# Gate and up weights in one tile, and their 256-column matmuls merged into 512-column ones

## Chip, cores and metric

One core of a Trainium2 chip. The metric is the device time of one execution in microseconds (us), lower is better. The kernel before takes 268.47 us (median of 3 runs, 268.25 to 269.01).

## The reference

An S5 layer (a diagonal complex recurrence over 2048 tokens of 1024 values) and a small mixture step are applied to the layernorm of x, and everything is added up. The change touches only the mixture step: a router picks 2 of the 2048 tokens, and a gated expert with an inner width of 3584 runs on these two rows.

```python
def _B_ref(x, w_r, w_gate, w_up, w_down):        # x: the layernorm's output, (1, 2048, 1024)
    r = x @ w_r
    idx = jnp.argsort(-r, axis=-1)[:, :2]        # two tokens
    ...
    g = _silu(x_sel @ w_gate)                    # w_gate, w_up: 1024 x 3584, bf16
    u = x_sel @ w_up
    y = (g * u) @ w_down                         # w_down: 3584 x 1024
    ...                                          # times sigmoid(r), added into the two rows
    return x + upd.reshape(B, S, D)

xn = _layernorm(A_x)
return A_x + _A_ref(xn, ...) + _B_ref(xn, ...)   # _A_ref: the recurrence
```

## The kernel before

Two parts matter. The first is how the expert's matmuls are laid out. Only two rows of activations exist, padded to 32, so they would fill a quarter of the array's columns. The kernel therefore cuts the weight's columns into four pieces and lets each piece be multiplied in its own strip of 32 array columns (`tile_position=(0, 32 * q)`), with the activations as the stationary operand and the weights streaming. Gate and up are done in 14 blocks (`UPV`): three parts of 1024 weight columns, each in four steps of 256 of the 1024 inputs, and one part of 512 columns in two steps of 512 inputs. The down product follows in 7 blocks.

```python
NREP = 4
UPB = [(b, DH * 2, 2, DT // 2) for b in range(0, F - DH, 2 * DH)] + [(F - DH, DH, 4, DT // 4)]
UPV = [(i, k) for i, blk in enumerate(UPB) for k in range(blk[3])]
...
wpool = ctx.enter_context(tc.tile_pool(name="wpool", bufs=4))     # each tile 512 KB
...
def load_w(n):                                   # n even: gate, n odd: up, then down
    if n < NUP:
        (b, k), w = UPV[n // 2], (B_w_gate, B_w_up)[n % 2]
        f0, fw, nk, _ = UPB[b]
        wt = wpool.tile([128, nk, fw], BF16, name="wt", tag="w")
        nc.sync.dma_start(out=wt[:], in_=w[k * nk * 128:(k + 1) * nk * 128, f0:f0 + fw].rearrange(...))
    ...

def moe_gateup(v):                               # 16 (or 32) matmuls a block
    ...
    wt = [ms.pop(("w", 2 * v + m)) for m in range(2)]
    for a in range(nk):
        j = k * nk + a
        for m in range(2):                       # gate, up
            for q in range(NREP):                # four strips
                nc.tensor.matmul(out=ms["pG", b][32 * q:32 * q + 32, m, :], lhsT=ms["xselT"][:, j, :],
                                 rhs=wt[m][:, a, q * fq:(q + 1) * fq], start=(j == 0 and m == 0),
                                 stop=(j == DT - 1 and m == 1), tile_position=(0, 32 * q))
```

The second part is the order. A list scheduler, run when the kernel is built, takes each piece of work with an estimated duration, a key, its predecessors and the ring of buffers it needs, and from these decides where on each engine it stands. The keys have been tuned by hand and search (`ADJUST`). A changed estimate or ring can thus move other work.

```python
for n in range(NW):                              # 42 loads; mb: megabytes that hold the DMA queue
    add(("w", n), "SP", 0.8, lambda n=n: load_w(n), ..., key=20 + n,
        takes=[("w", n, [("mm", n // 2)])], mb=0.43)
for v in range(NV):                              # 21 blocks
    ...
    add(("mm", v), "PE", 0.55, ..., [("w", 2 * v), ("w", 2 * v + 1)] + src + ..., key=-40 + v)
```

Of the kernel before, what the change touches and what calls it, by code (L numbers as in the profile page):

```python
# [12 lines left out]
BF16 = mybir.dt.bfloat16  # L13
# [10 lines left out]
NREP = 4  # L24
# [54 lines left out]
class Plan:  # L79
# [10 lines left out]
    def add(self, name, eng, dur, fn, deps=(), key=0.0, takes=(), mb=0.0, lag=0.0):  # L90
        assert name not in self.tasks, name
        key += self.adjust.get(name[0], 0.0) + self.adjust.get(name, 0.0)
        self.tasks[name] = dict(eng=eng, dur=dur, fn=fn, deps=list(deps), key=key, takes=list(takes), mb=mb, lag=lag)
# [70 lines left out]
def kernel(  # L164
# [18 lines left out]
    nc = tc.nc  # L183

    ctx.enter_context(tc.manual_schedule())
    _, L, D = A_x.shape
# [5 lines left out]
    DT = D // 128  # L192
# [6 lines left out]
    UPB = [(b, DH * 2, 2, DT // 2) for b in range(0, F - DH, 2 * DH)] + [(F - DH, DH, 4, DT // 4)]  # L199
    UPV = [(i, k) for i, blk in enumerate(UPB) for k in range(blk[3])]  # L200
# [69 lines left out]

    pl = Plan(ADJUST)
    for tag, n in (("xt", 4), ("xn", 2), ("xnT", NF - 2), ("pT", 1), ("pB", 3), ("pY", 3), ("u", 2), ("v", 2), ("gf", 2),
                   ("gb", 2), ("hT", 3), ("xr", 2), ("xa", 1), ("ot", 2), ("w", 4)):
        pl.ring(tag, n)
    add = pl.add

# [146 lines left out]
    for i in range(NWARM):  # L423
        add(("warm", i), "PE", 0.224 if i < 24 else 0.15, keep_clock, [("warm", i - 1)] if i else [], key=100 + i,
            takes=[("pB", "warm", [("warm", NWARM - 1)])])
# [4 lines left out]
    for c in range(NCH):  # L430
# [28 lines left out]
        if c < PE_T:  # L459
            add(("Tpe", c), "PE", 0.48, lambda c=c: transpose_pe(c), [("apply", c)], key=ln - 10,  # L460
                takes=[("pY" if c < 4 and c % 2 else "pT", ("T", c), [("xnT", c)])] + ([("pY", ("T", 0), [("xnT0",)])] if c == 0 else []))
# [192 lines left out]

    xrp = ctx.enter_context(tc.tile_pool(name="xrp", bufs=2))
    outp = ctx.enter_context(tc.tile_pool(name="outp", bufs=2))
    wpool = ctx.enter_context(tc.tile_pool(name="wpool", bufs=4))


    v_tiles = {}  # L660
# [86 lines left out]
    for c in range(NCH):  # L747
        f = c // CPF
        for js in parts(c):
            k = js.start  # L750
            half = len(parts(c)) > 1
            d = (js.stop - js.start) / PT
# [12 lines left out]
            for ri in range(2):  # L765
# [3 lines left out]
                    takes=[gb_take] if c == NCH - 1 else [("gf", (c, k), [("gb", c, k, i) for i in range(2)] + cy[0] + cy[1])] if half else  # L769
# [5 lines left out]
            if c + 1 < NCH:  # L775
# [4 lines left out]
                takes=[("hT", c, [("Y", c, YLAST(c))])])  # L780
# [50 lines left out]
    for c in range(NCH):  # L831
        add(("xr", c), "SP", 0.8, lambda c=c: load_xr(c), key=c - 2, deps=[("B", PT - 1, 1)] if c < 4 else [("Y", c - 4, 0)],
            takes=[("xr", c, [("xa", c)])], mb=0.25)
# [6 lines left out]
        wd = [(d.stop - d.start) / DH for d in cols(c)]  # L840
# [18 lines left out]
    ms = moe_state  # L859
# [92 lines left out]
    def sel_xT():  # L952
# [20 lines left out]
        takes=[("xt", "mw", [("gT", len(UPB) - 1), ("mm", len(UPV) - 1)])])  # L973


    NUP = 2 * len(UPV)

    def load_w(n):
        if n < NUP:
            (b, k), w = UPV[n // 2], (B_w_gate, B_w_up)[n % 2]  # L980
            f0, fw, nk, _ = UPB[b]
            wt = wpool.tile([128, nk, fw], BF16, name="wt", tag="w")
            nc.sync.dma_start(out=wt[:], in_=w[k * nk * 128:(k + 1) * nk * 128, f0:f0 + fw].rearrange("(a di) f -> di a f", di=128))
        else:
            fp = n - NUP
            wt = wpool.tile([128, 2, D], BF16, name="wd", tag="w")
            nc.sync.dma_start(out=wt[:], in_=B_w_down[fp * 256:(fp + 1) * 256, :].rearrange("(a fi) d -> fi a d", fi=128))
        ms["w", n] = wt

    def moe_gateup(v):  # L990
        b, k = UPV[v]
        f0, fw, nk, kn = UPB[b]
        fq = fw // NREP
        if k == 0:
            ms["pG", b] = psum.tile([128, 2, fq], F32, name="pG", tag="T" if b % 2 else "misc")
        wt = [ms.pop(("w", 2 * v + m)) for m in range(2)]
        for a in range(nk):
            j = k * nk + a
            for m in range(2):
                for q in range(NREP):  # L1000
                    nc.tensor.matmul(out=ms["pG", b][32 * q:32 * q + 32, m, :], lhsT=ms["xselT"][:, j, :],  # L1001
                                     rhs=wt[m][:, a, q * fq:(q + 1) * fq], start=(j == 0 and m == 0), stop=(j == DT - 1 and m == 1),
                                     tile_position=(0, 32 * q))

    def moe_exp(b):
        e = ms["e"][:, 0:UPB[b][1] // NREP]
# [25 lines left out]
    def moe_down(v):  # L1032
        if v == 0:
            ms["pD"] = psum.tile([128, DQ], F32, name="pD", tag="misc")
        for h in range(2):
            wd = ms.pop(("w", NUP + 2 * v + h))
            for a in range(2):
                ft = 4 * v + 2 * h + a
                for q in range(NREP):
                    nc.tensor.matmul(out=ms["pD"][32 * q:32 * q + 2, :], lhsT=ms["guT"][:, ft, :],  # L1040
                                     rhs=wd[:, a, q * DQ:(q + 1) * DQ], start=(ft == 0), stop=(ft == FT - 1),
                                     tile_position=(0, 32 * q))
# [17 lines left out]
    NV = NW // 2  # L1060
    for n in range(NW):
        add(("w", n), "SP", 0.8, lambda n=n: load_w(n), [("C", NDH - 1, 1)], key=20 + n,
            takes=[("w", n, [("mm", n // 2)])], mb=0.43)
    for v in range(NV):
        up = v < len(UPV)
        if up:
            b, k = UPV[v]
            src = [("xT",)] + ([("gT", b - 2)] if b > 1 and k == 0 else [])
        else:
            src = sorted({("gT", min((4 * (v - len(UPV)) + i) // 8, len(UPB) - 1)) for i in range(4)})  # L1070
        add(("mm", v), "PE", 0.55, (lambda v=v: moe_gateup(v)) if up else (lambda v=v: moe_down(v - len(UPV))),
            [("w", 2 * v), ("w", 2 * v + 1)] + src + ([("mm", v - 1)] if v else []), key=-40 + v)
    for b, (f0, fw, nk, kn) in enumerate(UPB):
        last = max(v for v, bk in enumerate(UPV) if bk[0] == b)
        d = fw / (2 * DH)
# [5 lines left out]
        takes=[("xt", "ym", [("row_", q) for q in range(1, NREP)]), ("xt", "ymb", [("Y", NCH - 1, YLAST(NCH - 1))])])  # L1081
# [36 lines left out]
```

## Time and profile before

| | before |
|---|---|
| span of the profiled execution | 266.8 us |
| PE busy | 259.1 us (97%) |
| DVE busy | 243.1 us (91%) |
| first gate/up matmul (tile pG) starts | 152.57 us |
| last matmul of the kernel starts | 263.57 us |
| gate/up matmuls: 192 of 256 columns, 64 of 128 | 7.3 and 1.3 us busy |

In the lines of this document, PE is the matmul engine (TensorE), DVE the VectorE, ACT the ScalarE and SP the engine whose queue issues the loads. On DVE, u is the recurrence's input (from pB), v its rotation, gf and gb the result of the scans, hT the rotation back, which PE multiplies into pY; ot takes pY to the output. Chunks and blocks are counted from 0. "128*32 128x256 x192" is a form: the stationary operand is 128 by 32, the moving one 128 by 256, and there are 192. L1001 is the source line of the gate/up matmul, L629 the input product (pB), L815 and L808 the output product (pY), all three in the full-array form (128*128); L1021 (pU) is a transposition in that form too, L1040 or L1041 (pD) the down product in the strip form. The three lines on the gate/up matmuls, from the view of the groups by form, give busy time and mean duration in ns; PEld is the loading of the stationary operand:

```profile
L1001 PE MATMUL pG<-wt,mw 128*32 128x256 bf16 x192 | 7.3, 275 | 0.0
L1001 PE MATMUL pG<-wt,mw 128*32 128x128 bf16 x64 | 1.3, 220 | 0.0
L1001 PEld LDWEIGHTS <-mw 128*32 128x32 bf16 x256 | 5.0, 96 | 4.3 <-issue 4.2
```

These matmuls hold PE for less than 9 of 267 us, so the change works on 3% of the span. The two lines of the PE timeline that bound the part the change can move:

```profile
152.57 1.06 PE L1001 MATMUL pG<-wt,mw 128*32 128x256 bf16 x32
...
263.57 0.28 PE L817 MATMUL pY<-ymb,hot 2*128 2x256 bf16 x1
```

From start to start this **stretch** is 263.57 - 152.57 = 111.00 us. The 111.00 rests on one profile of the kernel before.

### The profile page before, as it was taken

What the parts mean: (1) busy time and instruction counts of PE and PEld (TensorE: products, weight loads), DVE (VectorE), ACT (ScalarE), POOL (GpSimd) and SP (SyncE); (2) the same over time, 40 slices, a digit from 0 to 9 for tenths busy, and PEclk for the clock granted to TensorE, in tenths of its full rate; (3) what the DMA queues carried; (4) which work ended last, traced back from release to release, by engine and by line L of the source; (5) the groups of instructions that cost most, each with busy time, mean ns of one, the idle gap of its engine ahead of it and who ended that gap; (6) DMA issues with size and microseconds to landing.
All of it is one profiled execution on the core that took longest, in us unless ns stands there. A gap on an engine that the chain in (4) does not pass through costs nothing.

```text
span 266.8 us, 5838 instructions
## 1 busy us (share of the span) xinstructions
PE 259.1 (97%) x2373; PEld 176.9 (66%) x2373; DVE 243.1 (91%) x325; ACT 158.4 (59%) x281; POOL 86.9 (33%) x126
## 2 busy tenths in 40 slices
PE   6989999999999999979999999999999999999995
PEld 6979998784685575768546665678545885444452
DVE  5899999999999989996999998659999999999962
ACT  2679999947999999997330437227124473216110
POOL 3232214265646226213091634006206053232200
PEclk9999999999999999999999999999999999999999
DMA  7999999999621433133031188686779877751211
GB/s 178 182 169 194 222 228 209 277 223 354 189 76 73 122 100 103 57 81 99 1 97 43 59 277 294 210 314 217 270 225 307 256 270 270 271 197 55 88 40 39
DMA packets 66023, 46.26 MB, mean 173 GB/s; under 512 B 45829, under 2 KB 52107, under 8 KB 65997
## 3 DMA queue, kind: packets, MB, share of 16 engines
q1 hardware_dynamic: 65644, 45.56, 62.0%
q8 instruction: 18, 0.29, 0.5%
q0 software_dynamic: 144, 0.27, 0.3%
q10 hardware_dynamic: 208, 0.07, 0.1%
q14 instruction: 9, 0.07, 0.1%
HBM read 30.68 MB, written 4.20 MB: 131 GB/s over the span
## 4 chain that ended last, share of the span: by engine, by line
PE 54%; ACT 20%; DVE 17%; issue 3%; SPq 3%; DMA 2%; ACTq 0%
PE pY L815 29%; PE pB L629 18%; DVE gf L701 4%; ACT xn L347 4%; ACT xn L341 3%; ACT gb L707 3%; PE pG L1001 3%; SPq L284 2%; ACT xn L365 2%; PE pY L808 2%; ACT xa L793 2%; ACT u L635 2%; DVE v L680 2%; DMA xt<-in_A_x_dram 2%; DVE m L681 2%
## 5 line engine op out<-in xcount | busy, mean ns | idle before, releaser
L815 PE MATMUL pY<-CT,hT 128*128 128x512 bf16 (+1 forms) x528 | 118.6, 373 | 0.0
L629 PE MATMUL pB<-xnT,BT 128*128 128x256 bf16 (+1 forms) x1088 | 117.0, 266 | 1.4 <-ACT u L635 1.4
L629 PEld LDWEIGHTS <-BT 128*128 128x128 bf16 x1088 | 99.9, 98 | 14.5 <-issue 2.7
L717 POOL TENSOR_TENSOR cw<-gf,tL 128x16 f32<-128x16 f32 (+1 forms) x38 | 38.4, 1011 | 134.2 <-DVE gf L701 133.3
L815 PEld LDWEIGHTS <-hT 128*128 128x128 bf16 x528 | 49.0, 98 | 49.4 <-issue 1.3
L701 DVE TENSOR_TENSOR_SCAN gf<-R,v 128x1040 f32<-128x1040 f32 (+1 forms) x38 | 69.0, 1851 | 0.2
L635 ACT CAST u<-pB 128x512 bf16<-128x512 f32 x64 | 36.1, 581 | 22.3 <-PE pB L629 20.5
L707 ACT CAST gb<-gf 128x1024 bf16<-128x1024 f32 (+1 forms) x38 | 32.3, 862 | 24.6 <-DVE gf L701 24.5
L793 ACT ACTIVATE xa<-xr,nmr_all,rstd_all 128x1024 f32<-128x1024 bf16 x16 | 19.8, 1240 | 31.9 <-DVE ot L824 31.9
L824 DVE TENSOR_TENSOR ot<-pY,xa 128x512 bf16<-128x512 f32 (+1 forms) x33 | 21.9, 666 | 5.8 <-PE pY L817 4.5
L680 DVE TENSOR_TENSOR v<-u,E1c 128x2048 bf16<-128x2048 bf16 (+2 forms) x22 | 20.3, 924 | 5.4 <-ACT u L635 5.3
L742 DVE TENSOR_TENSOR hT<-gb,E2c 128x2048 bf16<-128x2048 bf16 (+2 forms) x22 | 20.4, 927 | 1.0 <-ACT gb L707 1.0
L682 DVE TENSOR_TENSOR v<-v,m 128x2048 bf16<-128x2048 bf16 (+2 forms) x22 | 20.6, 938 | 0.8
L744 DVE TENSOR_TENSOR hT<-hT,m 128x2048 bf16<-128x2048 bf16 (+2 forms) x22 | 20.6, 934 | 0.8
L681 DVE TENSOR_TENSOR m<-u,E1s 128x2048 bf16<-128x2048 bf16 (+2 forms) x22 | 20.5, 933 | 0.0
L743 DVE TENSOR_TENSOR m<-gb,E2s 128x2048 bf16<-128x2048 bf16 (+2 forms) x22 | 20.4, 927 | 0.0
L347 ACT ACTIVATE xn<-xt,nmean_all 128x1024 bf16<-128x1024 bf16 x12 | 13.8, 1149 | 0.2
L808 PEld LDWEIGHTS <-xnT 128*128 128x128 bf16 x128 | 9.0, 98 | 6.2 <-issue 2.7
L732 POOL CAST v<-cy 128x16 bf16<-128x16 f32 (+1 forms) x19 | 12.7, 668 | 1.2
L808 PE MATMUL pY<-dgD,xnT 128*128 128x128 bf16 x128 | 12.6, 220 | 0.2 <-DVE ot L824 0.2
L365 ACT ACTIVATE xn<-xt,nmr_all,rstd_all 128x1024 bf16<-128x1024 bf16 x10 | 12.4, 1241 | 0.3
L341 ACT ACTIVATE xn<-xt 128x1024 bf16<-128x1024 bf16 x12 | 12.6, 1049 | 0.0
(146 smaller groups left out, 178.1 us busy)
## 6 DMA issues: line engine op xcount, KB each, us to landing
wt<-in_B_w_gate_dram SPq DMA_DIRECT2D x14, 512.0 KB, 5.8
wt<-in_B_w_up_dram SPq DMA_DIRECT2D x14, 512.0 KB, 5.0
wd<-in_B_w_down_dram SPq DMA_DIRECT2D x14, 512.0 KB, 4.3
xt<-in_A_x_dram SPq DMA_DIRECT2D x16, 256.0 KB, 3.5
xr<-in_A_x_dram SPq DMA_DIRECT2D x16, 256.0 KB, 3.1
out_dram<-ot SPq DMA_DIRECT2D x31, 128.0 KB, 2.8
xnT<-xn SPq DMA_TRANSPOSE x10, 2.7
BT<-in_A_B_re_dram SPq DMA_TRANSPOSE x8, 4.8
```

Source lines behind the costliest of these rows:

```text
L347: nc.scalar.activation(out=xn_tiles[c][:], in_=xt_tiles[c][:], func=ACT.Square, bias=nmean_all[:, c:c + 1], accum_out=ln_part[c][:, 1:2])
L629: nc.tensor.matmul(out=pB[:, ri, ts_], lhsT=BT[ri][j][:, k, :], rhs=xnT_tiles[f][:, k, ts_], start=(k == 0), stop=(k == DT - 1))
L635: nc.scalar.copy(out=u_tiles[f][:, :, j, :], in_=pB_tiles.pop((f, j))[:])
L680: nc.vector.tensor_tensor(out=rot, in0=u, in1=both(E1c, js), op=ALU.mult)
L681: nc.vector.tensor_tensor(out=m[:, :, js, :], in0=u[:, ::-1], in1=E1s[:, :, js, :], op=ALU.mult)
L701: nc.vector.tensor_tensor_scan(out=flat(gf), data0=flat(R[:, js, :]), data1=flat(v[:, ri, js, :]), initial=0.0, op0=ALU.mult, op1=ALU.add)
L707: nc.scalar.copy(out=gb_tiles[c][:, ri, js, :], in_=gf_tiles[c, js.start, ri][:, :, 2:])
L717: nc.gpsimd.tensor_tensor(out=cw_tiles[c, js.start][:, ri, :, 0:n], in0=g.unsqueeze(1).to_broadcast([128, 2, n]), in1=tL[:, ri, :, js], op ...
L793: nc.scalar.activation(out=xa[:], in_=y_tiles.pop(("xr", c))[:], func=ACT.Identity, bias=nmr_all[:, c:c + 1], scale=rstd1_all[:, c:c + 1])
L808: nc.tensor.matmul(out=pY[:, j * 128:(j + 1) * 128], lhsT=xnT_tiles[f][:, k, ts_], rhs=dgD[:, k, :], start=(j == 0), stop=False)
L815: nc.tensor.matmul(out=pY[:], lhsT=h_tiles[c][:, ri, j, :], rhs=CT[ri][h][:, j, d0:d0 + w], start=False, stop=end)
L824: nc.vector.tensor_add(out=y_tiles["ot", c][:, d_], in0=y_tiles.pop(("pY", c, dh))[:], in1=y_tiles["xa", c][:, d_])
```

## The change

The intent is fewer and longer matmuls: gate and up of a block are loaded side by side into one tile, and one matmul streams both, 2 x 256 columns. 192 matmuls of 256 columns become 96 of 512, 64 of 128 become 32 of 256, and half of the loads of the stationary operand go. The pool has two pair tiles in place of four single ones, the same memory, and the scheduler's estimate of a block goes from 0.55 to 0.53 us (gate/up) or 0.6 us (down).

```diff
-    wpool = ctx.enter_context(tc.tile_pool(name="wpool", bufs=4))
+    wpool = ctx.enter_context(tc.tile_pool(name="wpool", bufs=2))
...
     def load_w(n):
-        ...
-            wt = wpool.tile([128, nk, fw], BF16, name="wt", tag="w")
+        v, m = divmod(n, 2)
+        ...
+        if ("w", v) not in ms:
+            ms["w", v] = wpool.tile([128, 2, nk, fw], BF16, name="wt", tag="w")
+        ...
+        nc.sync.dma_start(out=ms["w", v][:, m], in_=src.rearrange("(a p) f -> p a f", p=128))
...
-            for m in range(2):
-                for q in range(NREP):
-                    nc.tensor.matmul(out=ms["pG", b][32 * q:32 * q + 32, m, :], lhsT=ms["xselT"][:, j, :],
-                                     rhs=wt[m][:, a, q * fq:(q + 1) * fq], start=(j == 0 and m == 0), stop=(j == DT - 1 and m == 1),
-                                     tile_position=(0, 32 * q))
+            for q in range(NREP):
+                nc.tensor.matmul(out=ms["pG", b][32 * q:32 * q + 32], lhsT=ms["xselT"][:, j, :],
+                                 rhs=wt[:, :, a, q * fq:(q + 1) * fq], start=(j == 0), stop=(j == DT - 1),
+                                 tile_position=(0, 32 * q))
...
-            takes=[("w", n, [("mm", n // 2)])], mb=0.43)
+            takes=[("w", n // 2, [("mm", n // 2)])], mb=0.43)
...
-        add(("mm", v), "PE", 0.55, ...
+        add(("mm", v), "PE", 0.53 if up else 0.6, ...
```

More of the change, by code (lines that the diff above doesn't have):

```diff
@@ L272 @@
     for tag, n in (("xt", 4), ("xn", 2), ("xnT", NF - 2), ("pT", 1), ("pB", 3), ("pY", 3), ("u", 2), ("v", 2), ("gf", 2),
-                   ("gb", 2), ("hT", 3), ("xr", 2), ("xa", 1), ("ot", 2), ("w", 4)):
+                   ("gb", 2), ("hT", 3), ("xr", 2), ("xa", 1), ("ot", 2), ("w", 2)):
         pl.ring(tag, n)
@@ L978, in load_w @@
     def load_w(n):
-        if n < NUP:
-            (b, k), w = UPV[n // 2], (B_w_gate, B_w_up)[n % 2]
-            f0, fw, nk, _ = UPB[b]
-            wt = wpool.tile([128, nk, fw], BF16, name="wt", tag="w")
-            nc.sync.dma_start(out=wt[:], in_=w[k * nk * 128:(k + 1) * nk * 128, f0:f0 + fw].rearrange("(a di) f -> di a f", di=128))
-        else:
-            fp = n - NUP
-            wt = wpool.tile([128, 2, D], BF16, name="wd", tag="w")
-            nc.sync.dma_start(out=wt[:], in_=B_w_down[fp * 256:(fp + 1) * 256, :].rearrange("(a fi) d -> fi a d", fi=128))
-        ms["w", n] = wt
+        v, m = divmod(n, 2)
+        up = n < NUP
+        b, k = UPV[v] if up else (0, 0)
+        f0, fw, nk, _ = UPB[b] if up else (0, D, 2, 0)
+        if ("w", v) not in ms:
+            ms["w", v] = wpool.tile([128, 2, nk, fw], BF16, name="wt", tag="w")
+        if up:
+            src = (B_w_gate, B_w_up)[m][k * nk * 128:(k + 1) * nk * 128, f0:f0 + fw]
+        else:
+            src = B_w_down[(n - NUP) * 256:(n - NUP + 1) * 256, :]
+        nc.sync.dma_start(out=ms["w", v][:, m], in_=src.rearrange("(a p) f -> p a f", p=128))
     def moe_gateup(v):
@@ L995, in moe_gateup @@
             ms["pG", b] = psum.tile([128, 2, fq], F32, name="pG", tag="T" if b % 2 else "misc")
-        wt = [ms.pop(("w", 2 * v + m)) for m in range(2)]
+        wt = ms.pop(("w", v))
         for a in range(nk):
             j = k * nk + a
-            for m in range(2):
-                for q in range(NREP):
-                    nc.tensor.matmul(out=ms["pG", b][32 * q:32 * q + 32, m, :], lhsT=ms["xselT"][:, j, :],
-                                     rhs=wt[m][:, a, q * fq:(q + 1) * fq], start=(j == 0 and m == 0), stop=(j == DT - 1 and m == 1),
-                                     tile_position=(0, 32 * q))
+            for q in range(NREP):
+                nc.tensor.matmul(out=ms["pG", b][32 * q:32 * q + 32], lhsT=ms["xselT"][:, j, :],
+                                 rhs=wt[:, :, a, q * fq:(q + 1) * fq], start=(j == 0), stop=(j == DT - 1),
+                                 tile_position=(0, 32 * q))
     def moe_exp(b):
@@ L1034, in moe_down @@
             ms["pD"] = psum.tile([128, DQ], F32, name="pD", tag="misc")
+        wt = ms.pop(("w", NUP // 2 + v))
         for h in range(2):
-            wd = ms.pop(("w", NUP + 2 * v + h))
+            wd = wt[:, h]
             for a in range(2):
@@ L1070 @@
             src = sorted({("gT", min((4 * (v - len(UPV)) + i) // 8, len(UPB) - 1)) for i in range(4)})
-        add(("mm", v), "PE", 0.55, (lambda v=v: moe_gateup(v)) if up else (lambda v=v: moe_down(v - len(UPV))),
+        add(("mm", v), "PE", 0.53 if up else 0.6, (lambda v=v: moe_gateup(v)) if up else (lambda v=v: moe_down(v - len(UPV))),
             [("w", 2 * v), ("w", 2 * v + 1)] + src + ([("mm", v - 1)] if v else []), key=-40 + v)
```

## The prediction

> **What bounds the kernel now.** The instructions concerned all stand late in the kernel: the tile pG, which gate and up are summed in, is first written at 152.6 us of a span of 266.8 and the last weight matmul (pD, the down part) starts at 241.5 (the view of the tiles). I therefore read first the busy time of the engines in stretches from 145 us on. Its columns are the stretch, its length, then busy time and instruction count of each engine, the clock, the DMA share and GB/s.
>
> ```profile
> 145.00:170.00 25.00, 25.00 (x235) 15.04 (x233) 24.04 (x27) 10.97 (x16) 9.53 (x10) 1.00 0.58 200
> 170.00:205.00 35.00, 35.00 (x349) 23.01 (x338) 29.46 (x28) 13.99 (x21) 10.69 (x10) 1.00 0.77 252
> 205.00:242.00 37.00, 37.00 (x404) 23.34 (x402) 36.17 (x37) 14.15 (x20) 11.31 (x15) 1.00 0.71 246
> 242.00:264.00 22.00, 21.85 (x129) 11.19 (x127) 17.22 (x28) 5.43 (x7) 1.93 (x1) 1.00 0.16 55
> ```
>
> PE is busy in every microsecond up to 242 and nearly so to 264. Busy can hide a pause shorter than a pipelined matmul, so the waits of PE from 147 to 264 us came second: that answer is empty. The chain that ended last (third) runs on PE alone from 118.8 us to 263.9. So from there the end is the sum of PE's slots; DVE, 36 of 37 us busy in the third stretch, is the engine that could take over. The weight loads are a stream beside it. What one block of these matmuls costs is read from the timeline around one of them (start, length, form, count):
>
> ```profile
> 168.66 1.03 PE L815 MATMUL pY<-CT,hT 128*128 128x512 bf16 x4
> 169.62 0.62 PE L1001 MATMUL pG<-wt,mw 128*32 128x256 bf16 x16
> 170.17 5.42 PE L629 MATMUL pB<-xnT,BT 128*128 128x256 bf16 x48
> 175.51 0.62 PE L1001 MATMUL pG<-wt,mw 128*32 128x256 bf16 x16
> ```
>
> A block of sixteen takes 170.17 - 169.62 = 0.55 us, 34 ns for each matmul, though one lasts 273 ns: the 128*32 form puts four at a time beside each other, one in each strip of 32 columns. Two blocks in a row, and blocks in the narrow form, are in the next two views (chain, timeline):
>
> ```profile
> 152.64 0.99 PE pG L1001 x32
> ...
> 160.91 0.55 PE pG L1001 x16
> ```
> ```profile
> 213.17 0.63 PE L1001 MATMUL pG<-wt,mw 128*32 128x128 bf16 x32
> 213.63 0.61 PE L1040 MATMUL pD<-wd,guT 128*2 128x256 bf16 x16
> 214.17 1.05 PE L629 MATMUL pB<-xnT,BT 128*128 128x256 bf16 x8
> ```
>
> The second block of a pair adds only 0.99 - 0.55 = 0.44 us, that is 110 ns for each four of 256 columns, and this is the same 109 ns that one full-array matmul of 256 columns takes (5.34 us / 48 = 111 with its edges). So a run of four-strip matmuls is a stream of columns plus a fixed cost for going in and out of the form. That cost: in a narrower window the last full-array matmul of 512 columns starts at 169.31 and the first strip at 169.62, where two full-array ones stand 0.216 apart. From 169.31 to the pB start at 170.17 are 0.86 us; less that 512 slot (0.216) and four groups of 0.109 remain **0.21 us for each run**.
>
> **What the Trainium skill says.** (1) "TensorEngine Tiling (Array Packing)", Tiling Modes, Key Properties: changing the tiling mode drains the engine. The trace agrees, with 0.21 us for the way in and out. (2) "TensorE: Matmul & The Clock Gate", Part 1, "Wait — 56ns, not 53.3ns?": warm matmuls start N/2.4 GHz plus about 2.5 ns apart. The trace agrees: 1.73 us for eight of 512 columns is 216 ns. (3) The same page, Part 3, "Measured speedup vs the span model": packed tiles start about 4 ns apart. The timeline shows all four of the first group begun between 169.62 and 169.64. (4) "PSUM — Partial Sum Buffer", The four PSUM rules: a matmul's output fits one bank, 512 fp32 columns. The tile of gate and up, 2 x 256 fp32, is exactly one, so the merge is legal; this is no time.
>
> **The change part by part.** *Merging.* 192 matmuls of 256 columns become 96 of 512, and 64 of 128 columns become 32 of 256; as many weight loads go. But columns streamed stay equal: a block was four groups of 256, now two of 512. Only the 2.5 ns per group goes: 12 blocks x 2 groups x 2.5 ns = 0.06 us, and the two narrow blocks had eight groups and have four: 2 x 4 x 2.5 = 0.02 us. Weight loads (5.0 us busy before) stood beside the matmuls, as the pitch of 109 shows, so they give nothing. **Gain 0.08 us.**
>
> *The order of instructions.* The kernel's list scheduler gets new durations and a pair of weights as one buffer, and places the rest anew. I compared the two built programs. PE is the same up to 170 us. Then block 5 stands one pB step (sixteen matmuls, 1.75 us) earlier; the last gate/up block (13) and the down blocks come between other pB and pY work; and block 13, which stood next to the first down block (the view at 213.17), now stands alone. Before, 21 blocks made 19 runs (blocks 0 and 1, and 13 and the first down, adjoin); after, 20 runs. **Cost 1 x 0.21 us.** From the chunk 13/14 outputs on (some 242 us) all engines have the old order.
>
> *Loads.* Size, number and queue are unchanged (28 of 512 KB for gate and up). A pair is now freed and refilled together, and the first matmul of a block waits for both halves instead of for gate alone, the up half following 0.1 us later. The halves were sometimes issued apart before (up of block 5 not until 170.17, used at 175.51); now together at 164.0.
>
> Sum: -0.08 + 0.21 = **+0.13 us**, 268.47 to 268.6.
>
> **The rivals.**
> *A: a load turns into a wait of PE.* I took each pair's issue as the end of the block that frees its buffer, and its use from the sum of PE's slots in the new order. The gaps are 7 to 10 us, the shortest that of the sixth down block (about 230.5 to 236.9 us, 6.4) and of block 12 (gate half at 198.3, used at 205.4, as before). The view of the weight tiles gives 3.8/5.1/7.1 us from issue to landing (least, median, most) for gate and up, and 3.7/4.3/7.3 for down; the long ones had four loads in line. So a wait is possible only in bad luck: up to 1 us, each. Against it: before had gaps of 5.3 us and no wait.
> *B: DVE becomes the bound.* Block 5 now stands ahead of the last pB of its group, so u comes 0.65 us later, and DVE starts this chunk's rotation 0.65 us later than here:
>
> ```profile
> 176.24 1.23 DVE L680 TENSOR_TENSOR v<-u,E1c 128x2048 bf16<-128x2048 bf16 x1 [5.04 <-ACT u L635]
> ```
>
> DVE then has no pause until 201.9, so it runs late by up to 0.65 us. In the new order its next piece waits for the exponentials of gate (ACT ends them at 203.1), where the delay is swallowed. Adding DVE's durations from there (hT 3.53, scan pair 4.45, v 3.6, ot 0.6) I get hT of chunks 12 and 13 done at 221.1 and 231.0; PE uses them at 231.2 and 235.5. The scan of chunk 14 starts at 235.9 (235.69 before), and its hT is done by 245.6, used at 247.4. The smallest gaps are 0.8 to 1.8 us. If a duration grows by contention, PE would wait some tenths: 269 to 269.5.
> *C: the merge saves real time.* If the 34 ns per matmul were an issue cost, halving the count would save 14 x 0.27 = 3.8 us (264.7, still only 1.4%). Against it: the narrow form runs 32 in 0.46 us (213.17 to 213.63), 14 ns each, so issue does not bind at 34.
> *D: streaming two pieces of 512 bytes, 4 KB apart, for one matmul is slower.* Nothing in this profile has that form as the moving side; ten per cent would be 14 x 0.04 = 0.6 us.
>
> **Range and chances.** The centre is 268.6. The runs of before spread from 268.25 to 269.01, so about 0.4 either way is noise. Below, only C in part; above, A, B and D with up to 1 us. Eight in ten: 267.9 to 269.8. Faster by 2% (263.1) would need more than all 14 blocks can give up even under C; slower by 2% is 273.8, five waits of 1 us. Chances 0.01, 0.97, 0.02.
>
> **What would show the steps right or wrong.** A block of 8 matmuls of 512 columns standing alone takes 0.55 us from its start to the next full-array start (C: 0.3 to 0.4; D: 0.6 or more); two in a row about 0.98. Half the weight loads of these blocks (128 of 256) are gone, with no time to show for it. 20 runs of strips instead of 19. No wait of PE from 150 to 264 us: a wait on a weight tile would be A, one on DVE's hT or ot B. The rotation of 176.24 starts near 176.9 and the hT of chunk 14 ends near 245.6. The prediction falls if PE's waits in that stretch add up to over 1 us.

## The result, and the profile after

The changed kernel's median is 269.12 us (268.32 to 269.70, 6 runs), against 268.38 us (268.25 to 269.01, 6 runs) before. The ratio is 1.002, with a 95% interval of 0.9999 to 1.004: the same at the 2% that counts here. Ratios in this document are the mean time of one kernel's fast runs over that of the other's of the same rounds, so they are not quite the ratio of the medians quoted. The profiled executions have the same span, 266.8 us.

The groups by form after the change:

```profile
L1001 PE MATMUL pG<-wt,mw 128*32 128x512 bf16 x96 | 7.2, 384 | 0.0
L1001 PE MATMUL pG<-wt,mw 128*32 128x256 bf16 x32 | 1.2, 275 | 0.0
L1001 PEld LDWEIGHTS <-mw 128*32 128x32 bf16 x128 | 2.2, 95 | 4.1 <-issue 3.4 <-DMA wt<-in_B_w_up_dram 0.4
```

Half the matmuls and half the stationary loads are gone, and PE's busy time on them fell by 0.2 us of 8.6. (The 0.4 us for which PEld stood idle until a load landed, at 163.30, cost nothing: PE was on pY until then and went on after its usual 0.31 us.) A single matmul became longer, 384 ns for 275. The PE timeline shows a lone block, then the part around the first down block:

```profile
169.47 0.61 PE L1001 MATMUL pG<-wt,mw 128*32 128x512 bf16 x8
170.02 3.67 PE L629 MATMUL pB<-xnT,BT 128*128 128x256 bf16 x32
...
209.48 0.62 PE L1001 MATMUL pG<-wt,mw 128*32 128x256 bf16 x16
210.04 1.92 PE L629 MATMUL pB<-xnT,BT 128*128 128x256 bf16 x16
211.79 0.39 PE L808 MATMUL pY<-dgD,xnT 128*128 128x128 bf16 x4
212.02 1.89 PE L815 MATMUL pY<-CT,hT 128*128 128x512 bf16 x8
213.74 0.22 PE L1021 MATMUL pU<-ident,mw 128*128 128x128 bf16 x1
213.89 0.61 PE L1041 MATMUL pD<-wt,guT 128*2 128x256 bf16 x16
...
218.12 1.91 PE L629 MATMUL pB<-xnT,BT 128*128 128x256 bf16 x16
219.96 0.61 PE L1041 MATMUL pD<-wt,guT 128*2 128x256 bf16 x16
```

A block of 8 takes 170.02 - 169.47 = 0.55 us from its start to the next one's, as the block of 16 did. At 209.48 the last gate/up block stands alone; before, the first down block followed it at once. This is the one extra change into and out of the strip form. The ends of the stretch:

```profile
152.45 1.05 PE L1001 MATMUL pG<-wt,mw 128*32 128x512 bf16 x16
...
263.58 0.28 PE L817 MATMUL pY<-ymb,hot 2*128 2x256 bf16 x1
```

263.58 - 152.45 = 111.13 us, 0.13 us more than before. Two neighbours stayed clear of the path: DVE, whose rotation began 0.5 us later than before (176.74 for 176.24) and whose hT of chunk 14 still ended in time, and the weight loads, whose time from issue to landing (least, median, most) grew at its upper end. The first two lines are from the DVE timeline, the third is the view of the weight tiles:

```profile
176.74 1.23 DVE L680 TENSOR_TENSOR v<-u,E1c 128x2048 bf16<-128x2048 bf16 x1 [5.69 <-ACT u L635]
...
244.30 1.22 DVE L744 TENSOR_TENSOR hT<-hT,m 128x2048 bf16<-128x2048 bf16 x1
```
```profile
DMA to landing us min/median/max: 3.9/5.5/8.3
```

The view of PE's waits from 147 to 264 us is empty again. In the stretches, the third (205 to 242 us) has PE busy for 37.00 of 37.00 us with 371 matmuls in place of 404, and DVE for 36.61 us (36.17 before):

```profile
205.00:242.00 37.00, 37.00 (x371) 23.09 (x370) 36.61 (x37) 14.15 (x20) 13.30 (x15) 1.00 0.72 244
```

### The profile page after: what moved, and what is told of

Same layout as the page of the kernel before. It is cut to its first block, busy times and chain, and to the rows that moved or that the text cites. A ratio compares the mean times of both kernels' runs of the same rounds, so it can differ in the third digit from the quotient of the medians.

```text
span 266.8 us, 5572 instructions
## 1 busy us (share of the span) xinstructions
PE 260.1 (97%) x2245; PEld 175.1 (66%) x2245; DVE 242.9 (91%) x325; ACT 158.4 (59%) x281; POOL 87.2 (33%) x126
## 4 chain that ended last, share of the span: by engine, by line
PE 54%; ACT 20%; DVE 17%; issue 3%; SPq 2%; DMA 2%; ACTq 0%
PE pY L815 29%; PE pB L629 18%; DVE gf L701 4%; ACT xn L347 4%; ACT xn L341 3%; ACT gb L707 3%; PE pG L1001 3%; ACT xn L365 2%; PE pY L808 2%; ACT xa L793 2%; SPq L284 2%; DMA xt<-in_A_x_dram 2%; ACT u L635 2%; DVE v L680 2%; DVE m L681 2%
```

## The experiments

**The theory (S, streaming and runs).** A block's time is the columns that stream through four strips, which the merge does not change, plus 0.21 us for each *run* of strip-form matmuls between full-array ones. The merge gives 0.08 us; the new order has one run more (20 for 19) and takes 0.21. **Rivals:** the merge saves real issue time and something else took it (C); the longer two-piece matmul is slower in itself (D); weight loads became a wait on the path (A). All outputs are right. "Stretch" is the one defined above, from each profiled execution.

| kernel | what differs from the changed kernel | median us | ratio to before (95%) | stretch us | S expects |
|---|---|---|---|---|---|
| before | | 268.38 | | 111.00 | |
| after | | 269.12 | 1.0020 (0.9999 to 1.0040) | 111.13 | 111.13 |
| again | nothing | 269.08 | 1.0008 (0.9988 to 1.0029) | 111.13 | 111.13 |
| unmerged | 256-column matmuls | 268.75 | 1.0006 (0.9988 to 1.0024) | 111.21 | 111.21 |
| adjacent | last gate/up block next to first down block | 268.79 | 1.0006 (0.9985 to 1.0026) | 111.09 | 110.92 |
| switch | a full-array matmul inside each block | 271.80 | 1.0114 (1.0089 to 1.0139) | 114.25 | 114.5 |
| strip | the same in strip form, run once | 269.19 | state unknown | 111.61 | 111.5 |
| narrow64 | 64 matmuls of 64 columns a block | 270.16 | 1.0055 (1.0036 to 1.0074) | 112.55 | 111.6 |
| fifteenruns | 15 runs | 269.13 | 1.0015 (0.9992 to 1.0038) | 111.07 | 110.08 |
| twelveruns | 12 runs | 270.88 | 1.0078 (1.0059 to 1.0097) | 113.37 | 109.45 |
| tenruns | 11 runs (10 were expected), loads estimated shorter throughout | 286.11 | 1.0651 (1.0636 to 1.0667) | 127.07 | not a test |
| thirteenruns | 14 runs (13 were expected), likewise | 287.04 | 1.0678 (1.0653 to 1.0704) | 128.69 | not a test |

### again: the changed kernel, unaltered, in five rounds

Edit: none.

> The changed kernel once more, unaltered, to see whether the 0.7 us between the medians of the first six runs is real. Theory (one more run of strips, all else equal): the stretch from the first pG matmul to the last pY matmul (111.00 us before, 111.13 after) is again 111.1 us, the median lies within 0.3 us of that of before (ratio 1.000 to 1.001), and its runs spread no wider than 0.8 us. Rival (in some executions a block waits for its weights, which landed only 0.4 us before use in the first profile): the ratio is again 1.002 or more, single runs reach 269.5 us, and if this profile falls on such a run it shows a wait on a weight tile.

Measured: 269.08 us against 268.55 us (11 runs), ratio 1.0008 with 1 inside the interval; stretch 111.13 us, the same to 0.01 us. The first pG matmul started at 153.32 us here and at 152.45 us in the first profile, with the same program. So a scatter of 0.9 us lies ahead of the stretch, and the difference of medians (0.7 us in the first set, 0.5 us here) cannot be put down to the stretch that the change alters. Whether any of it beyond 0.13 us is real, these runs do not settle. Two of the expectations missed: the medians lie 0.5 us apart, not within 0.3, and the runs spread over 1.2 us, not 0.8 (those of before over 1.4 here). The rival, a wait for weights in the slower executions, fails all the same: this profile fell on such a one (269.47 us), and shows no wait on a weight tile and the same stretch.

### unmerged: the new order with the old matmuls

```diff
-            for q in range(NREP):
-                nc.tensor.matmul(out=ms["pG", b][32 * q:32 * q + 32], ..., rhs=wt[:, :, a, q * fq:(q + 1) * fq], ...)
+            for m in range(2):
+                for q in range(NREP):
+                    nc.tensor.matmul(out=ms["pG", b][32 * q:32 * q + 32, m, :], ..., rhs=wt[:, m, a, q * fq:(q + 1) * fq], ...)
```

> The changed kernel with its order, its pair buffers and its loads, but each matmul of 512 columns split again into two of 256 (256 instead of 128 matmuls on gate and up). Theory: a block standing alone takes 0.645 us over the full-array slot instead of 0.641, so the stretch from the first pG to the last pY is 111.21 us (0.08 more than 111.13) and the time is that of the changed kernel within noise. Rival C (the count of matmuls costs): 128 more at 34 ns each make it 4.4 us longer, 1.6%. Rival (the moving side in two pieces of 512 bytes is slower): it would be shorter than the changed kernel.

Its stretch runs from 153.02 to 264.23 us, 111.21 us. This splits the change in two by measurement: order and loads alone 111.21 - 111.00 = +0.21 us, the merge alone 111.13 - 111.21 = -0.08 us. Both are the terms that the prediction's sum has. A lone block from the PE timeline of this kernel:

```profile
170.06 0.62 PE L1002 MATMUL pG<-wt,mw 128*32 128x256 bf16 x16
170.61 0.61 PE L629 MATMUL pB<-xnT,BT 128*128 128x256 bf16 x4
```

Sixteen matmuls take 0.55 us, as the eight of the changed kernel do. Rivals C and D fall here: the same order with twice the matmuls differs by 0.006 us a block.

### switch and strip: what a change of form costs

In each of the 14 blocks, half-way, one matmul of one column is put in. It multiplies by a column of zeros, so the sums stay right. In *switch* it is full-array, in *strip* it is in the first strip.

```diff
+            if a == nk // 2:      # switch
+                nc.tensor.matmul(out=ms["pG", b][:, 0, 0:1], lhsT=ident[:], rhs=ms["xselT"][:, j, 2:3], start=False, stop=False)
```
```diff
+            if a == nk // 2:      # strip
+                nc.tensor.matmul(out=ms["pG", b][0:32, 0, 0:1], lhsT=ms["xselT"][:, j, :], rhs=ms["xselT"][:, j, 2:3],
+                                 start=False, stop=False, tile_position=(0, 0))
```

> The changed kernel with one full-array matmul of a single zero column between the two halves of each of the 14 gate and up blocks (the sum is unchanged), so that each block goes out of the strip form and in again: 14 more ways out and in. Theory: each costs 0.21 us plus some 0.03 us for the added matmul, 14 x 0.24 = 3.4 us: about 272.0 us, 1.3% slower, all of it between the first pG and the last pY (114.5 us). Rival (the way in and out is hidden or is an artefact of how ends of matmuls are recorded): the 14 added matmuls cost 0.03 us each, 0.4 us in all.

> The control of the run named switch: the same added matmul of one zero column between the halves of each gate and up block, but in the strip form (one strip) instead of over the full array, so that nothing goes out of the form. Theory: 14 x 0.03 = 0.4 us, the stretch from the first pG to the last pY is 111.5 us (111.13 without, 114.25 with the full-array one). Rival (any matmul between the halves costs it, not the change of form): 114.2 again.

One block of *switch* in the PE timeline, from the last full-array matmul ahead of it:

```profile
170.12 0.38 PE L815 MATMUL pY<-CT,hT 128*128 128x512 bf16 x1
170.43 0.40 PE L1003 MATMUL pG<-wt,mw 128*32 128x512 bf16 x4
170.76 0.18 PE L1001 MATMUL pG<-mw,ident 128*128 128x1 bf16 x1
170.87 0.40 PE L1003 MATMUL pG<-wt,mw 128*32 128x512 bf16 x4
171.20 1.05 PE L629 MATMUL pB<-xnT,BT 128*128 128x256 bf16 x8
```

And one of *strip*:

```profile
169.32 0.38 PE L815 MATMUL pY<-CT,hT 128*128 128x512 bf16 x1
169.62 0.40 PE L1004 MATMUL pG<-wt,mw 128*32 128x512 bf16 x4
169.85 0.17 PE L1001 MATMUL pG<-mw 128*32 128x1 bf16 x1
169.85 0.40 PE L1004 MATMUL pG<-wt,mw 128*32 128x512 bf16 x4
170.19 1.05 PE L629 MATMUL pB<-xnT,BT 128*128 128x256 bf16 x8
```

From the last full-array matmul to pB, switch needs 171.20 - 170.12 = 1.08 us and strip 170.19 - 169.32 = 0.87 us; the changed kernel needs 0.86. The second half of a strip block starts 0.23 us after the first (169.62 to 169.85), in switch 0.44 us (170.43 to 170.87). So it is the change of form that costs, not one more matmul. Over the whole stretch switch adds 114.25 - 111.13 = 3.12 us, that is 0.223 us for each of 14; strip adds 0.48, of which 0.26 is a single wait on a weight load at 201.4 us (by the starts of the matmuls), leaving 0.22, or 0.015 us for each. The change of form alone is then 0.223 - 0.015 = 0.21 us. This is the strongest evidence for the 0.21 us a run: the cost was put in 14 times and showed 14 times. What takes the time inside it is not told apart: the array may run empty, or the new form's first stationary load may come too late (in the kernel before it starts at 169.61 us, with the first strip at 169.62, after PEld had stood idle for 0.42 us).

### narrow64: 64 matmuls in a block in place of 8

```diff
+            cw = 64
+            for m in range(2):
+                for i in range(fq // cw):
+                    for q in range(NREP):
+                        nc.tensor.matmul(out=ms["pG", b][32 * q:32 * q + 32, m, i * cw:(i + 1) * cw], ...)
```

> The changed kernel with each matmul of 512 columns cut into eight of 64 (1024 instead of 128 on gate and up), order and loads unchanged. Theory (a block is a stream of columns plus 2.5 ns for each group of four strips, and the count does not matter until the weight loads or the start of a matmul bind): 12 blocks x 14 more groups x 2.5 ns + 2 x 12 x 2.5 = 0.5 us more, 269.1 us, same. Rival C (each matmul costs its 34 ns of issue): 896 x 34 ns = 30 us more. Between (a weight load of 32 columns cannot be hidden behind 64 columns): some microseconds, with the weight loads busy through the whole block.

A block from its PE timeline:

```profile
169.99 0.69 PE L1004 MATMUL pG<-wt,mw 128*32 128x64 bf16 x64
170.61 0.61 PE L629 MATMUL pB<-xnT,BT 128*128 128x256 bf16 x4
```

64 matmuls take 0.62 us where 8 take 0.55. If each matmul had a cost of its own of 34 ns, 56 more would have added 1.9 us to the block; they added 0.07. The stretch grew by 1.42 us. By the starts of the matmuls, twelve blocks took 0.073 us more each (0.88), the two that adjoin 0.20 together, and one wait on a load inside the last gate/up block 0.34, which is all of it. S expected 14 more groups of four strips in a block to cost 2.5 ns each, 0.5 us in all; the blocks cost 1.08 us, some 5 ns a group. So C falls by a factor of more than 20, and the cost of 2.5 ns a group is a little too low for short ones.

### adjacent: one run of strips taken back

The last gate/up block is made to wait for the first down pair too, so the scheduler puts the two next to each other again: 19 runs.

```diff
+    PAIR = lambda v: v == 13
...
-            [("w", 2 * v), ("w", 2 * v + 1)] + src + ([("mm", v - 1)] if v else []), key=-40 + v)
+            [("w", 2 * v), ("w", 2 * v + 1)] + ([("w", 2 * v + 2), ("w", 2 * v + 3)] if PAIR(v) else [])
+            + src + ([("mm", v - 1)] if v else []), key=-40 + v)
```

> The changed kernel, with the last gate and up block made to wait for the first down pair too, so that the two stand next to each other again, as in the kernel before: 19 runs of strips instead of 20. Theory: the stretch from the first pG to the last pY falls by 0.21 us, from 111.13 to 110.92, less than before's 111.00; the time falls by 0.2 us, which may drown in the spread. Rival (the 0.13 us came from something else in the new order, not from the number of runs): 111.1 stays.

The stretch came out at 111.09 us, 0.17 above the 110.92 expected. The place is in its PE timeline:

```profile
218.67 1.91 PE L629 MATMUL pB<-xnT,BT 128*128 128x256 bf16 x16
220.68 0.61 PE L1041 MATMUL pD<-wt,guT 128*2 128x256 bf16 x16
```

From the pB start to the second down block are 2.01 us; in the changed kernel (218.12 to 219.96) the same sixteen matmuls and the same step take 1.84 us. The run saved was given back as this pause of 0.17 us. The two loads of that block were issued from 214.61 us, 6.1 us before use; in the changed kernel from 210.15 us, 9.8 us before. The pause is too short for the view of the waits, but the chain of the work that ended last (start, length, what) runs through one of these loads, so it is a wait on weights:

```profile
214.61 0.38 SPq L989
...
215.03 5.61 DMA wt<-in_B_w_down_dram
...
220.68 0.61 PE pD L1041 x16
```

Without it the stretch would be 110.92 us, as S expects.

### fifteenruns and twelveruns: many runs taken back

The same rule as in *adjacent* for more blocks, with a shorter estimate of how long a load holds the queue, from the fifth load on, so the scheduler accepts it. The first four loads keep theirs, and with them the early order.

```diff
+    PAIR = lambda v: v in (4, 6, 8, 10, 13)              # fifteenruns, mb=0.43 if n < 4 else 0.36
+    PAIR = lambda v: v in (5, 7, 9, 11, 13, 15, 17)      # twelveruns,  mb=0.43 if n < 4 else 0.33
```

> The same with fewer pairs (4 and 5, 6 and 7, 8 and 9, 10 and 11, 13 and the first down block): 15 runs. Theory: 111.44 - 5 x 0.21 = 110.4 us for that stretch, 1.05 us less than the changed kernel, ratio to before 0.997. Rivals as in twelveruns.

> The mended form of tenruns, whose changed load estimate had reshuffled the whole kernel ahead of the weights too: the estimate is now left alone for the first four loads, so that all engines have the changed kernel's order until its third block. Seven pairs of blocks (5 and 6 to 17 and 18) are taken together: 12 runs of strips. Theory (0.21 us for each run): the stretch from the last pY ahead of the first pG to the last pY is 111.44 - 8 x 0.21 = 109.8 us, the time 1.7 us less than the changed kernel, 267.1 us, ratio to before 0.994. Rival A (loads): the runs of two stand 8.9 us or more apart by their matmuls and four loads in line landed in 7 to 8.3 us, so at most some tenths come back. Rival B (the new order makes PE wait for DVE, as in tenruns): waits for hT, 268 us or more.

Neither is faster than before; twelveruns is 0.8% slower. The waits of PE in the stretch, in us (sum, count, longest), of fifteenruns and then of twelveruns:

```profile
PE pG L1001 <- DMA wt<-in_B_w_gate_dram: 0.5, 1, 0.5
PE pD L1041 <- DMA wt<-in_B_w_down_dram: 0.3, 1, 0.3
```
```profile
PE pG L1001 <- DMA wt<-in_B_w_up_dram: 1.6, 1, 1.6
PE pD L1041 <- DMA wt<-in_B_w_down_dram: 1.4, 2, 1.0
PE pY L808 <- DVE ot L824: 0.3, 1, 0.3
```

The view counts a wait only from the modelled end of the matmul before. By the starts of the matmuls, less their usual distance, the two waits of fifteenruns are 0.53 and 0.40 us and the stretch without them is 111.07 - 0.93 = 110.14 us; S expects 111.13 - 5 x 0.21 = 110.08. For twelveruns the four waits are 1.80, 0.60, 1.02 and 0.50 us in the same way, 3.9 together, and 113.37 - 3.9 = 109.5 us; S expects 111.13 - 8 x 0.21 = 109.45. So the saving of a run is real, and the price is mostly a wait on weights: two blocks in a row consume both pair tiles, and a refill, whose loads take up to 7.9 and 6.6 us to land in these two, can start only then. A third pair tile might ease it, but each takes 8 KB of every partition, and a build with a larger pool was refused, with 16.125 KB left for it, which holds two; so that could not be tried.

### tenruns and thirteenruns: a spoilt order

The same rule with the shorter estimate on all loads (mb=0.36).

```diff
+    PAIR = lambda v: v % 2 == 0 and v + 1 < NV          # tenruns
+    PAIR = lambda v: v in (2, 4, 6, 8, 10, 13)          # thirteenruns
...
-            takes=[("w", n // 2, [("mm", n // 2)])], mb=0.43)
+            takes=[("w", n // 2, [("mm", n // 2)])], mb=0.36)
```

> The changed kernel with gate, up and down blocks taken two at a time (the first of each two waits for both, and the scheduler is told that a load takes less of the queue): 10 runs of strips instead of 20, with the same buffers and the same loads, which are now issued four in line. Theory (a fixed 0.21 us for each run): 10 x 0.21 = 2.1 us less, 266.4 us, ratio to before 0.993, if no block has to wait for its loads; the stretch from the last pY matmul ahead of the first pG to the last pY is 109.3 us instead of 111.44. Rival A (loads): four in line took 7 to 8 us to land, the shortest distance between two runs is now 7.6 us (the second) and 5.8 us (the last, with two loads), so PE may wait some tenths at those and give part of the gain back: 266.6 to 267.5 us.

> The same for the first five pairs of gate and up blocks and for the last gate and up block with the first down block alone: 13 runs of strips. Theory: 7 x 0.21 = 1.5 us less than the changed kernel, 267.1 us, ratio to before 0.995. Rival A: waits for loads give back some tenths, less than with ten runs.

Both are over 6.5% slower, a clear miss. Their expectations also counted one run too few: pairing 21 blocks leaves 11 runs, and 14 in thirteenruns, as their PE timelines show. PE's largest waits from 118 us on in tenruns:

```profile
PE pY L815 <- DVE xnsel L944: 7.3, 1, 7.3
PE pY L815 <- DVE hT L744: 5.4, 2, 5.0
```

PE waits for the normalised rows of the router and for hT, hardly for weights (0.2 us in tenruns, 1.3 in thirteenruns). The shorter estimate had changed the order long before the first block: PE's timelines of tenruns and of the changed kernel part at some 80 us. Pairing and estimate were changed together here. A build of the changed kernel with the estimate as its only edit has PE's order of tenruns up to the first block, so that early order comes from the estimate; its time was not measured. The granted clock was 0.93 from 118 to 150 us and 0.91 from 150 to 200; what that took is not separated. These two kernels do not test S; they led to the two above, where the early estimate is left alone.

## Why the prediction was right

**Total.** 268.6 us was predicted; 269.12 and 269.08 us were measured, inside the range and the same within 2%. The part that was worked out, +0.13 us, is what the stretch shows: 111.00 to 111.13 us, twice. For the remaining 0.4 to 0.6 us of the median the profiles show no place in the stretch, and the intervals of both sets of runs (barely, in the first) include no difference at all.

**The merge, 0.08 us.** Right: unmerged against after gives 0.08 us. The count of columns decides, not the count of matmuls. The half of the stationary loads that went (5.0 to 2.2 us busy) gave no time.

**One more run, 0.21 us.** Right: unmerged against before gives 0.21 us, and switch gives 0.223 us for each change put in.

**Rival A, a load wait.** The prediction was right that none would come, but it was closer than told. The up halves of two early pairs landed 0.4 us ahead of use (block 2 at 160.27 for 160.70 us, block 3 at 162.90 for 163.30), with the longest load at 8.3 us in place of the 7.1 us that the profile before shows and the prediction counted with. The same order showed one wait each, of 0.26 and 0.34 us, in strip and narrow64, so that none came here is in part luck.

**Rival B, DVE.** Right that DVE would start late and PE would not wait: the rotation starts at 176.74 us (176.9 predicted), and the hT of chunk 14 ends by about 245.44 us (245.6), where the next DVE instruction starts, as before. One reading was wrong: DVE did have short pauses before 201.9 us (its timeline of the kernel before stands still for some 0.1 us ahead of ot at 192.51 and 196.85), so most of the delay was made up before the place where the prediction has it swallowed: ot of 201.90 us started at 202.02.

**Rivals C and D.** Refuted: 0.55 us for a lone block and 0.98 us for two in a row, as the centre had it; C wanted 0.3 to 0.4, D 0.6 or more.

**What the prediction left out.** It counted the run as a cost of the change and did not ask what taking runs back would give. That is 0.21 us each, but in *adjacent* and *fifteenruns* most of it, and in *twelveruns* more than all of it, was given back in waits, nearly all of them for weights.

No version tried beats the kernel before.

## What to carry to other kernels

Before merging matmuls, find out what a block of them is made of: here it is streamed columns plus a fixed price for each change between full-array and strip form, so halving the count gave 0.08 us, and one more change of form took 0.21. Count the runs of the unusual form, in the built order and not in the source, and set the buffers that longer runs need against what they save. In a kernel ordered by a scheduler with tuned keys, treat every estimate as part of the tuning: the two kernels with the loads' estimate changed throughout (and blocks paired) came out over 6.5% slower.

## What the Trainium skill lacked or had wrong

- "TensorEngine Tiling (Array Packing)", Tiling Modes, Key Properties: it says that a change of mode drains the engine and gives no size. Here one way in and out costs 0.21 us, by the extra run (unmerged against before), and 0.223 us by the full-array matmul added 14 times; the same matmul kept in strip form cost 0.015.
- "TensorE: Matmul & The Clock Gate", Part 2, "Back-to-back issue gap": it gives a sustained 81 ns for a matmul of 128 columns and 131 ns for one of 512 in a stream with weight loads. Here four of 128 take 212.02 - 211.79 = 0.23 us, some 57 ns each, and 512-column ones 216 ns each, each with its own weight load; its formula for the isolated case fits both.
- The same page, Part 3, "The mechanism": its summary of what overlaps has weight loads beside matmuls in flight only where the row group differs (a sentence above it also allows a background weight buffer). Here the matmuls of pB use all 128 rows, and sixteen of 256 columns, each with a weight load of 98 ns, start within 211.79 - 210.04 = 1.75 us, 109 ns apart, so the loads overlap.
